# The first query block's first 512 keys under a bound of their own

## The chip, the cores and the metric

One core of one Trainium2 chip. The metric is device microseconds (us) of one execution; a time given here is the median of some executions, and a span is what the profile of one execution covers (about 1.8 us less than its time). Engines: PE multiplies matrices, ACT (ScalarE) does the exponentials, DVE (VectorE) and POOL (GpSimd) do elementwise work, SP issues most transfers. PE leaves its results in banks of PSUM (named PD, PO and PA); ACT and DVE copy them out from there, which the texts call evacuation.

## The reference, cut to what matters

```python
B, S, D, H = 1, 2048, 448, 16          # Dh = 28
qkv = (x @ wqkv).reshape(B, S, 3, H, Dh).transpose(2, 0, 3, 1, 4)
q, k, v = qkv[0], qkv[1], qkv[2]
scores = jnp.einsum("bhqd,bhkd->bhqk", q, k) * (Dh ** -0.5)
p = jax.nn.softmax(scores, axis=-1)
o = jnp.einsum("bhqk,bhkd->bhqd", p, v)
out = o.transpose(0, 2, 1, 3).reshape(B, S, D) @ wo
```

Everything is bfloat16. There are 16 heads x 2048 queries x 2048 keys, so 67 million exponentials.

## The kernel before

Heads are taken in 4 groups of 4, queries in blocks of 512. Scores are computed with keys on the partitions. The kernel does not take the true maximum over keys but an upper bound: for each dimension the largest absolute key value (KMAX) times the absolute query value, summed over the dimensions. The bound rides in the same matmul: each head has 32 spare rows, which hold minus the margin times KMAX on the key side (KB) and |q| on the query side (QB). The exponentials are split: most tiles go to ACT, two at a time (128x1024, named PTA), the others run through a polynomial on DVE and POOL (names DU, DV, DG, PTD).

The consequence for the start: no score can be formed before the maxima of **all** 2048 keys of the group are known, hence not before the whole input has been loaded, transposed and projected to keys.

```python
# setup: four x blocks by SP, weights of K and Q by ACT's queue
for b in range(NQC):
    nc.sync.dma_start(out=XS[b][:], in_=x_perm[:, b * TPC:(b + 1) * TPC, :])
for (W, off) in ((WK, D), (WQ, 0)):
    nc.scalar.dma_start(out=W[:, :, 0:GW], in_=wq3[:, :, off:off + GW])
# ...
nc.vector.memset(maskm[:], -MARG)
nc.vector.tensor_scalar(out=maskm[:], in0=maskm[:], scalar1=maskcol[:, 0:1], ...)
# ... memsets of VA and WO on DVE, then the first transfers of WO

# each x block: PE transposes, DVE copies one half to XT_0, ACT the other to XT_1
# K of group 0, four chunks (sc) of 512 keys: 4 matmuls, maximum on DVE, copy on ACT
red = nc.vector.tensor_reduce(out=KPART[g][:, sc:sc + 1], in_=ap(), op=ALU.max, apply_absolute_value=True)
nc.scalar.activation(out=KB[0][pr][:, cs], in_=ap(), func=ACT.Identity, bias=onescol[:, 0:1], scale=1.0)
# ... after all four chunks
nc.vector.tensor_reduce(out=KMAX[g][:], in_=KPART[g][:], op=ALU.max)
# bound rows of KB (32x512, x4 for the first chunk) and of QB (|q|, x4)
nc.vector.tensor_scalar(out=KB[0][i // 2][...], in0=maskm[...], scalar1=KMAX[g][...], op0=ALU.mult)
nc.vector.tensor_scalar(out=qb[i // 2][...].bitcast(U16), in0=qb[i // 2][...].bitcast(U16), scalar1=0x7FFF, op0=ALU.bitwise_and)
```

The order of instructions on every engine is fixed when the program is built, by a small list scheduler inside the kernel that works with estimated durations (the numbers 0.585, 0.61 and so on in the diff below) and a priority for each operation. A few constants (DI, QEA, PARTU) steer it. A plan is an order and not a clock: if an instruction comes late, all behind it on its engine come late, even if they could have run (in the changed kernel Q's copy on ACT stood behind a K copy that waited 0.82 us for DVE, and started 2.3 us behind the first K copy; with that K copy moved behind it, in run g0, 0.8 us).

## Time and profile before

| | before |
|---|---|
| time, median | 415.06 us; 414.88 beside the changed kernel |
| span of the profiled execution | 413.1 us |
| ACT busy | 400.0 us, 97% |
| first exponential starts | 16.38 us |
| fourth exponential starts | 19.45 us |
| last of 424 exponentials starts / ends | 404.28 / 405.56 us |
| ACT's wait ahead of the last copies | 3.06 us |

The profile's page for the kernel before: span, busy time, ACT and PE clock in 40 slices of the span (9 is 90% or more), and the chain of waits.

```profile
span 413.1 us, 7525 instructions
PE 362.4 (88%) x2605; PEld 121.4 (29%) x2617; DVE 394.0 (95%) x696; ACT 400.0 (97%) x439; POOL 224.1 (54%) x203
...
ACT  4999999999999999999999999999999999999994
...
PEclk9999999999999999999999999999999999999999
...
ACT 86%; issue 8%; PE 2%; DMA 2%; DVE 1%; SPq 0%; DVEq 0%; ACTq 0%
```

ACT is full in every slice but the first and the last, and 86% of the chain that ended last lies on it. So the time is made of three parts: when ACT's stream starts, how much work lies in it, and the tail behind it. DVE at 95% is nearly as full, which is why work cannot simply be handed to it.

ACT's timeline of the kernel before, around the start and at the end. The columns are start and length in us, engine, line, operation, output and input, count, and in brackets how long the engine sat idle before it and what released it.

```profile
14.29 0.69 ACT L474 ACTIVATE QB_0_85<-PD_201,offscol 128x512 bf16<-128x512 f32 x1 [0.24 <-PE PD_201 L466]
...
15.44 0.69 ACT L474 ACTIVATE QB_1_86<-PD_201,offscol 128x512 bf16<-128x512 f32 x1
16.38 1.02 ACT L903 ACTIVATE PTA_131<-PA_198 128x1024 bf16<-128x1024 f32 x1 [0.25 <-PE PA_198 L631]
...
19.45 1.03 ACT L903 ACTIVATE PTA_134<-PA_199 128x1024 bf16<-128x1024 f32 x1
...
404.28 1.28 ACT L903 ACTIVATE PTA_145<-PA_199 128x1024 bf16<-128x1024 f32 x1
408.61 0.53 ACT L1032 CAST OUTF_211<-PD_201 128x448 bf16<-128x448 f32 x1 [3.06 <-PE PD_201 L1027]
```

Exponentials follow each other at 0.917 us (the printed lengths overlap). Before the first ACT makes five K copies and two Q copies (the Q copies at 14.29 and 15.44 are shown, the first held up by PE); behind the last, ACT waits 3.06 us for the last block's normalisation and output matmuls.

DVE's timeline of the same kernel, the setup up to the first transpose copy:

```profile
3.19 0.35 DVE L231 TENSOR_SCALAR maskm<-maskm,maskcol 128x512 bf16<-128x512 bf16 x1
...
4.78 0.81 DVE L234 MEMSET WO<- 128x896 uint32 x1
5.50 0.21 DVE L286 COPY WKP_79<-WK 112x448 bf16<-112x448 bf16 x1
5.66 0.69 DVE L319 COPY XT_0_63<-PD_200 112x1024 bf16<-112x1024 bf16 x1
```

### The profile page before, as it was taken

What the parts mean: (1) busy time and instruction counts of PE and PEld (TensorE: products, weight loads), DVE (VectorE), ACT (ScalarE), POOL (GpSimd) and SP (SyncE); (2) the same over time, 40 slices, a digit from 0 to 9 for tenths busy, and PEclk for the clock granted to TensorE, in tenths of its full rate; (3) what the DMA queues carried; (4) which work ended last, traced back from release to release, by engine and by line L of the source; (5) the groups of instructions that cost most, each with busy time, mean ns of one, the idle gap of its engine ahead of it and who ended that gap; (6) DMA issues with size and microseconds to landing.
All of it is one profiled execution on the core that took longest, in us unless ns stands there. A gap on an engine that the chain in (4) does not pass through costs nothing.

```text
span 413.1 us, 7525 instructions
## 1 busy us (share of the span) xinstructions
PE 362.4 (88%) x2605; PEld 121.4 (29%) x2617; DVE 394.0 (95%) x696; ACT 400.0 (97%) x439; POOL 224.1 (54%) x203
## 2 busy tenths in 40 slices
PE   8988989898898889888898988979898888989995
PEld 4533232223232232322223222222322222222231
DVE  6899999999999999999999999999999999999975
ACT  4999999999999999999999999999999999999994
POOL 2155456464655556475465656547375656556450
PEclk9999999999999999999999999999999999999999
DMA  8410011202201001110400001010310101001012
GB/s 256 77 20 21 3 47 11 53 25 54 72 1 44 2 28 30 20 38 8 111 8 27 21 9 40 2 36 11 77 48 2 47 2 35 12 27 47 4 69 89
DMA packets 33413, 15.83 MB, mean 38 GB/s; under 512 B 26016, under 2 KB 30304, under 8 KB 33376
## 3 DMA queue, kind: packets, MB, share of 16 engines
q1 hardware_dynamic: 32304, 15.05, 14.5%
q8 instruction: 20, 0.33, 0.4%
q10 hardware_dynamic: 1072, 0.32, 0.3%
q14 instruction: 17, 0.14, 0.1%
HBM read 7.37 MB, written 1.96 MB: 23 GB/s over the span
## 4 chain that ended last, share of the span: by engine, by line
ACT 86%; issue 8%; PE 2%; DMA 2%; DVE 1%; SPq 0%; DVEq 0%; ACTq 0%
ACT PTA_131 L903 5%; ACT PTA_132 L903 4%; ACT PTA_133 L903 4%; ACT PTA_136 L903 4%; ACT PTA_135 L903 4%; ACT PTA_134 L903 4%; ACT PTA_145 L903 4%; ACT PTA_140 L903 4%; ACT PTA_139 L903 4%; ACT PTA_138 L903 4%; ACT PTA_137 L903 4%; ACT PTA_144 L903 4%; ACT PTA_142 L903 3%; ACT PTA_143 L903 3%; ACT PTA_141 L903 3%
## 5 line engine op out<-in xcount | busy, mean ns | idle before, releaser
L714 POOL TENSOR_TENSOR DG_181<-DV_175,DU_169 128x512 f16<-128x512 f16 x30 | 34.6, 1155 | 34.8 <-DVE DV_175 L711 34.6
L714 POOL TENSOR_TENSOR DG_182<-DV_176,DU_170 128x512 f16<-128x512 f16 x30 | 34.6, 1155 | 28.8 <-DVE DV_176 L711 28.7
L714 POOL TENSOR_TENSOR DG_184<-DV_178,DU_172 128x512 f16<-128x512 f16 x29 | 33.5, 1155 | 29.5 <-DVE DV_178 L711 28.2
L714 POOL TENSOR_TENSOR DG_186<-DV_180,DU_174 128x512 f16<-128x512 f16 x29 | 33.5, 1155 | 26.9 <-DVE DV_180 L711 26.7
L714 POOL TENSOR_TENSOR DG_185<-DV_179,DU_173 128x512 f16<-128x512 f16 x29 | 33.5, 1155 | 25.7 <-DVE DV_179 L711 25.6
L714 POOL TENSOR_TENSOR DG_183<-DV_177,DU_171 128x512 f16<-128x512 f16 x29 | 33.5, 1156 | 22.9 <-DVE DV_177 L711 22.7
L631 PEld LDWEIGHTS <-KB_1_94 64*128 64x128 bf16 x256 | 20.8, 92 | 48.4 <-issue 47.4
L631 PEld LDWEIGHTS <-KB_0_91 64*128 64x128 bf16 x256 | 20.5, 92 | 45.8 <-issue 42.1
L631 PEld LDWEIGHTS <-KB_1_92 64*128 64x128 bf16 x256 | 20.1, 93 | 45.8 <-issue 44.0
L631 PEld LDWEIGHTS <-KB_0_93 64*128 64x128 bf16 x256 | 20.3, 92 | 43.5 <-issue 42.5
L903 ACT ACTIVATE PTA_140<-PA_199 128x1024 bf16<-128x1024 f32 x18 | 22.4, 1247 | 0.0
L903 ACT ACTIVATE PTA_144<-PA_199 128x1024 bf16<-128x1024 f32 x18 | 22.4, 1245 | 0.0
L903 ACT ACTIVATE PTA_143<-PA_198 128x1024 bf16<-128x1024 f32 x18 | 22.3, 1241 | 0.0
L903 ACT ACTIVATE PTA_142<-PA_199 128x1024 bf16<-128x1024 f32 x18 | 22.3, 1239 | 0.0
L903 ACT ACTIVATE PTA_141<-PA_198 128x1024 bf16<-128x1024 f32 x18 | 22.3, 1236 | 0.0
L903 ACT ACTIVATE PTA_139<-PA_198 128x1024 bf16<-128x1024 f32 x17 | 21.1, 1241 | 0.0
L708 DVE TENSOR_SCALAR DU_171<-PD_202 128x512 f16<-128x512 uint16 x29 | 19.8, 682 | 1.0 <-PE PD_202 L631 0.7
L708 DVE TENSOR_SCALAR DU_172<-PD_200 128x512 f16<-128x512 uint16 x29 | 19.7, 681 | 0.9 <-PE PD_200 L631 0.9
L711 DVE SCALAR_TENSOR_TENSOR DV_178<-PD_200,DU_172 128x512 f16<-128x512 uint16 x29 | 19.8, 684 | 0.3
L711 DVE SCALAR_TENSOR_TENSOR DV_176<-PD_201,DU_170 128x512 f16<-128x512 uint16 x29 | 19.8, 683 | 0.2
L708 DVE TENSOR_SCALAR DU_169<-PD_200 128x512 f16<-128x512 uint16 x29 | 19.8, 682 | 0.2 <-PE PD_200 L631 0.2
L903 ACT ACTIVATE PTA_145<-PA_198 128x1024 bf16<-128x1024 f32 x16 | 20.0, 1247 | 0.0
(596 smaller groups left out, 1511.3 us busy)
## 6 DMA issues: line engine op xcount, KB each, us to landing
RRB_194<-SCR_196 SPq DMA_DIRECT2D x8, 256.0 KB
RRB_195<-SCR_197 SPq DMA_DIRECT2D x7, 256.0 KB
KB_1_94<-KB_0_93 SPq DMA_DIRECT2D x4, 128.0 KB
XS_127<-in_x_dram SPq DMA_DIRECT2D x1, 448.0 KB
XS_128<-in_x_dram SPq DMA_DIRECT2D x1, 448.0 KB
XS_129<-in_x_dram SPq DMA_DIRECT2D x1, 448.0 KB
XS_130<-in_x_dram SPq DMA_DIRECT2D x1, 448.0 KB
out_dram<-XS_127 SPq DMA_DIRECT2D x1, 448.0 KB
```

What stands on the lines that cost most here:

```text
L631: nc.tensor.matmul(out=ap, lhsT=KB[g % 2][i // 2][a:a + 64, j * P:(j + 1) * P], rhs=QB[w % NQB][i // 2][a:a + 64, :], start=True, stop=Tru ...
L708: p1 = add(Op("DVE", P1, lambda: nc.vector.tensor_scalar(out=DU[b][:], in0=lo, scalar1=SIG / 65536, scalar2=SIG * (SS - 0.5), op0=ALU.mult ...
L711: p2 = add(Op("DVE", P1, lambda: nc.vector.scalar_tensor_tensor(out=DV[b][:], in0=lo, scalar=65536 * (SS - 0.5 + CE / C3), in1=DU[b][:], o ...
L714: gq = add(Op("POOL", PTT, lambda: nc.gpsimd.tensor_tensor(out=DG[b][:], in0=DV[b][:], in1=DU[b][:], op=ALU.mult), deps=[p2], prio=n, kind ...
L903: nc.scalar.activation(out=PTA[pslot.idx][:, 0:len(ns) * QW], in_=PA[s.idx][:, 0:len(ns) * QW], func=ACT.Exp, bias=ACT_BIAS, scale=ACT_SCALE)
```

## The change

The intent is to start ACT's stream sooner. For the first query block the first 512 keys run under a bound made of **their own** maxima, so the first exponentials need only one K chunk and Q. The other 1536 keys of the block run under the bound of all maxima, as before. The two parts of the block then have value sums under different bounds; the first part is copied out, multiplied by exp(difference of the bounds), and added to the second.

To make this cheap the factors change sides: KB's bound rows become the constant minus the margin, and the query side holds |q| times the maxima. For group 0 that constant has to be written into four 32x1536 pieces of KB, which is done by POOL. The core of the diff (the cuts are marked; left out are mostly changed priorities and PSUM banks of the plan; Q's weights are now loaded by SP and their copy runs on ACT instead of POOL):

```diff
-    DI = 2
+    DI = 1
...
-    QEA = 30
+    QEA = 20
...
-    PARTU = 40
+    PARTU = 50
...
+    nc.vector.tensor_scalar(out=negm[:], in0=maskm[:, 0:HP], scalar1=-1.0, scalar2=None, op0=ALU.mult)
+    for pr in range(2):
+        for st in range(HG):
+            nc.gpsimd.memset(selcol[pr][HP * st:HP * (st + 1), :], 1.0 if st % 2 == pr else 0.0)
+        nc.vector.tensor_tensor(out=bndcol[pr][:], in0=onescol[:], in1=maskm[:, 0:1], op=ALU.subtract)
+        nc.vector.tensor_tensor(out=bndcol[pr][:], in0=bndcol[pr][:], in1=selcol[pr][:], op=ALU.mult)
+        nc.vector.tensor_tensor(out=bndcol[pr][:], in0=bndcol[pr][:], in1=maskm[:, 0:1], op=ALU.add)
+    for pr in range(2):
+        for st in range(HG):
+            if st % 2 != pr:
+                nc.gpsimd.memset(KB[0][pr][HP * st:HP * (st + 1), QW:S], -MARG)
...
-            evs = [add(Op("ACT", 0.585, lambda pr=pr: nc.scalar.activation(
-                out=KB[0][pr][:, cs], in_=ap(), func=ACT.Identity, bias=onescol[:, 0:1], scale=1.0),
-                deps=[ops[-1], red], ...)) for pr in range(2 if sc == 0 else 1)]
+            if sc == 0:
+                evs = [add(Op("ACT", 0.585, lambda pr=pr: nc.scalar.activation(
+                    out=KB[0][pr][:, cs], in_=ap(), func=ACT.Identity, bias=bndcol[pr][:, 0:1], scale=selcol[pr][:, 0:1]),
+                    deps=[ops[-1]], prio=-4480 if pr == 0 else -4360, lat=0.17)) ... for pr in range(2)]
...
+            else:      # chunks 1 to 3 go through KB[1] and are moved by DMA
+                evs = [add(Op("ACT", 0.585, lambda: nc.scalar.activation(out=KB[1][0][:, cs], ...)))]
...
+            for i in range(HG):    # first 512 keys: |q| times chunk 0's maxima
+                o = bound(qb, i, KPART[0], [ab, kmaxop[0][0], e1], ...)
+            for i in range(HG):    # the rest: |q| times all maxima
+                qev2[i] = bound(q2, i, KMAX[0], [cps[i // 2], ab, kmax_op[0]], ...)
...
+    def task_factor():
...
+        e = add(Op("ACT", 0.49, lambda: nc.scalar.activation(out=DT[:], in_=bank(task)[:], func=ACT.Exp, scale=ACT_SCALE), ...))
...
+    def finish_block():
+        ev = add(Op("DVE", 0.62, lambda: nc.vector.tensor_copy(out=RRB[1][:], in_=PO[:]), ...))
+        first_part.append(add(Op("POOL", 1.22, lambda: nc.gpsimd.tensor_tensor(out=RRB[1][:], in0=RRB[1][:], in1=DT[:], op=ALU.mult), ...)))
...
+            ev = add(Op("DVE", 0.62, lambda: nc.vector.tensor_tensor(out=OSB[b][:], in0=PO[:], in1=RRB[1][:], op=ALU.add), ...))
```

## The prediction

> **What bounds the kernel.** The exponentials on ACT. The page: ACT 97% busy, 86% of the chain that ended last; the stretches of busy time: ACT 100% from 21 to 395 us. In ACT's timeline the first exponential starts at 16.38 us, the 424th at 404.28: 0.917 us each, no gap but 0.33 us after the first. Then 8.8 us of tail. Time = start of the stream + ACT work inside it + tail.
>
> **Removed.** 16.38 us ends a chain: x block 2 lands at 7.94, transposes, all four K chunks (PE done 13.38), the last reduction of maxima (14.19), the overall maximum, two bound writes into KB (0.34 each), two into QB (0.28 each). The first block now needs only K chunk 0 and Q 0. Also gone from ACT before the stream: one transpose copy (0.9), one Q and three K evacuations (0.585 each).
>
> **Added or moved.** By the instruction order: the three K evacuations stand between the first exponentials (3 x 0.6); one exponential of the rescaling factor (about 0.5); 425 exponential pairs, not 424 (0.92), as DVE gets 174 tiles, not 176. Together 3.2 us more ACT work inside the stream. DVE gets seven small setup instructions ahead of the K weight copy (about 1.1 us: dependent DVE instructions follow each other at 0.2 us in the trace), four 32x512 bound multiplies (0.34) twice, copies of Q (0.28), one transpose copy, one copy of the partial sums (0.6), mostly paid for by two tiles fewer (3.6). Tail: same work.
>
> **The new start, by trace durations.** Setup moves XT_0_63 on DVE from 5.66 to about 6.7; K0 is done on PE about 9.1. [...] before's waits agree: ACT waited twice for DVE's maximum of the same bank (0.5 us in all). So evacuation, maximum and second evacuation of that bank alternate, ACT, DVE, ACT: 9.1, 9.8, 10.6. Q's evacuation ends about 11.8; absolute value, copy, a transpose copy and two bounds on DVE end about 13.7; first exponential about 14.1, 2.3 us earlier.
>
> Then the stream is not dense. The second K chunk's maximum stands on DVE behind two more bounds, two transpose copies and a copy, and ACT's next instruction waits for it: a hole of about 1.5 us after exponential 1. The fourth exponential starts about 20.2 (before: 19.45). Moving K chunks by DMA (issue 0.6 each, landing roughly 2 us) should be just in time.
>
> Balance: stream position +0.8, factor +0.5, one more exponential +0.9: +2.2 us by this count. The retuned constants may give some back, and the start is uncertain by 1.5 us, so I lower it to +1.1: 416.2 us, range 412.8 to 418.8. Faster by over 2%: 0.02; within: 0.95; slower: 0.03.
>
> **What would show it.** ACT's timeline: first exponential at 13 to 15 us; ACT idle 1 to 2 us between exponential 1 and the K evacuation, released by DVE's maximum; fourth exponential at 19 to 21; then 0.917 spacing; last exponential starting 8 to 9 us before the end. DVE: XT_0_63 at 6.5 to 7.
>
> **What would make it wrong.** GpSimd's four new memsets (32x1536) holding up DVE's fast copies: start later by 1 us or more. Plan skew: the order was fixed for earlier starts, so PE may hold ACT's scores behind tiles that wait for DVE: holes after 20 us, up to 419. If setup costs DVE less and the hole closes, 413.

The alternation rests on the two waits alone (0.21 and 0.25 us in the trace of the kernel before). The sum: 0.8 + 0.5 + 0.9 = 2.2 us, lowered to 1.1, on 415.06 us. The figures for DMA can be read in the same trace: the first copy of KB, issued at 15.58 us, took 0.63 us to issue, and its packets had landed at 17.46, 1.9 us after the start of the issue.

## More of the kernel before

The granted clock is the share of PE's full speed that the profile records.

The granted clock of PE from 8 to 14 us in the kernel before. The columns are the stretch, its length, busy us of PE, weight loads, DVE, ACT and POOL with counts, the PE clock as a share of full speed, the share of the DMA engines, GB/s.

```profile
8.00:14.00 6.00, 5.84 (x50) 3.66 (x51) 3.87 (x6) 4.91 (x7) 1.33 (x1) 1.00 0.80 155
```

## The result

The changed kernel takes 422.18 us (4 runs, 421.95 to 422.23), the kernel before 414.88 (4 runs, 414.65 to 415.25). The ratio is 1.0176, with a 95% interval of 1.0161 to 1.0190. Ratios here are the mean time of one kernel's runs over that of the other's of the same rounds, so not quite the ratio of the medians. The change made the kernel 1.8% slower; it lies outside the predicted range (412.8 to 418.8).

Its page, the same lines:

```profile
span 420.4 us, 7567 instructions
PE 364.9 (87%) x2617; PEld 122.4 (29%) x2617; DVE 397.3 (94%) x705; ACT 400.5 (95%) x440; POOL 227.7 (54%) x213
...
ACT  2599999999999999999999999999999999999993
...
PEclk8899999999999999999999999999999999999998
...
ACT 74%; PE 12%; DVE 6%; issue 6%; POOL 1%; POOLq 0%; ACTq 0%; DVEq 0%
```

ACT is busy for 400.5 us, only 0.5 more than before: the loss of 7.3 us of span is not work but waiting. It shows in the first slices (2 and 5 where there were 4 and 9), and the PE clock is below full there too. The chain of waits, 86% on ACT before, now runs through PE and DVE for 18%.

ACT's timeline of the changed kernel:

```profile
12.73 0.78 ACT L429 ACTIVATE KB<-PD,bndcol,selcol 128x512 bf16<-128x512 f32 x1 [5.64 <-PE PD L418]
14.33 0.78 ACT L429 ACTIVATE KB<-PD,bndcol,selcol 128x512 bf16<-128x512 f32 x1 [0.82 <-DVE KPART L425]
15.00 0.68 ACT L529 ACTIVATE QB<-PD,offscol 128x512 bf16<-128x512 f32 x1
...
18.03 1.02 ACT L1018 ACTIVATE PTA<-PA 128x1024 bf16<-128x1024 f32 x1 [0.17 <-PE PA L700]
20.60 0.69 ACT L438 ACTIVATE KB<-PD,onescol 128x512 bf16<-128x512 f32 x1 [1.55 <-DVE KPART L425]
...
24.31 1.93 ACT L1018 ACTIVATE PTA<-PA 128x1024 bf16<-128x1024 f32 x2
...
389.49 22.37 ACT L1018 ACTIVATE PTA<-PA 128x1024 bf16<-128x1024 f32 x24
415.75 0.53 ACT L1147 CAST OUTF<-PD 128x448 bf16<-128x448 f32 x1 [3.89 <-PE PD L1142]
```

The first exponential starts at 18.03 us, not 2.3 us earlier than before but 1.65 later. Ahead of it ACT waits 5.64 us for the first K chunk from PE. The 1.55 us hole behind the first exponential was predicted and is there. The last exponential ends at 389.49 + 22.37 = 411.86, and ACT then waits 3.89 us, 0.83 more than before.

The 7.3 us of span divide exactly into three stretches, each read off these timelines:

| stretch | before | after | difference |
|---|---|---|---|
| span's start to the fourth exponential's start | 19.45 | 24.31 | +4.86 |
| from there to the last exponential's end | 386.11 | 387.55 | +1.44 |
| last exponential's end to the span's end | 7.54 | 8.54 | +1.00 |

The middle one is one more exponential (425, 0.92 us) and the exponential of the factor (about 0.5). The three rows are used below as start, work and tail.

Why the first K chunk is so late shows on DVE (the changed kernel's timeline, the instructions shown of before and the new one ahead of them):

```profile
3.20 0.35 DVE L245 TENSOR_SCALAR maskm<-maskm,maskcol 128x512 bf16<-128x512 bf16 x1
3.59 1.31 DVE L246 TENSOR_SCALAR negm<-maskm 128x32 bf16<-128x32 bf16 x1
...
7.13 0.81 DVE L259 MEMSET WO<- 128x896 uint32 x1
7.86 1.42 DVE L311 COPY WKP<-WK 112x448 bf16<-112x448 bf16 x1
9.20 0.67 DVE L350 COPY XT<-PD 112x1024 bf16<-112x1024 bf16 x1
```

and on POOL, in the same stretch:

```profile
3.37 5.77 POOL L256 MEMSET KB<- 32x1536 bf16 x4
```

A multiplication of 128x32 elements took 1.31 us, and the copy of the K weights, 0.21 us before, took 1.42. Both ended just when one of POOL's four memsets of 1.44 us ended: 3.37 + 1.44 = 4.81 against 4.90, and 3.37 + 5.77 = 9.14 against 9.28. The first transpose copy XT_0_63 stands behind them on DVE at 9.20 us instead of 5.66.

And PE, which needs that copy for the first K matmuls, sat idle. The changed kernel's PE timeline and its clock in the stretch shown of before:

```profile
9.92 1.01 PE L418 MATMUL PD<-XT,WKP 112*128 112x512 bf16 x2 [4.34 <-DVE XT L350]
```

```profile
8.00:14.00 6.00, 4.08 (x16) 2.22 (x17) 3.02 (x4) 0.78 (x1) 1.14 (x1) 0.50 0.71 146
```

PE waited 4.34 us, and from 8 to 14 us its granted clock was half of full speed. Two matmuls of the K chunk took 1.01 us where two took 0.60 before.

So there is a chain of three suspects: POOL's memsets hold up DVE's short instructions (0.21 us grew to 1.42); PE idles (4.34 us) and its clock falls (to 0.50); and the plan's order, made for earlier starts, leaves holes. The traces suggest it. The runs below test it.

### The profile page after: what moved, and what is told of

It is laid out like the page before. It is cut to its first block, busy times and chain, and to the rows that moved or that the text cites. A ratio compares the mean times of both kernels' runs of the same rounds, so it can differ in the third digit from the quotient of the medians. Undisturbed runs are those within 1.5% of the kernel's fastest.

```text
span 420.4 us, 7567 instructions
## 1 busy us (share of the span) xinstructions
PE 364.9 (87%) x2617; PEld 122.4 (29%) x2617; DVE 397.3 (94%) x705; ACT 400.5 (95%) x440; POOL 227.7 (54%) x213
## 4 chain that ended last, share of the span: by engine, by line
ACT 74%; PE 12%; DVE 6%; issue 6%; POOL 1%; POOLq 0%; ACTq 0%; DVEq 0%
ACT PTA L1018 73%; PE PA L700 5%; PE PO L871 3%; PE PD L700 1%; DVE DV L816 1%; DVE DU L813 1%; DVE XT L350 1%; PE PO L418 1%; DVE PTD L832 0%; PE PD L418 0%; PE PO L521 0%; PE PO L587 0%; ACT KB L429 0%; DVE QB L541 0%; DVE WKP L311 0%
## 5 line engine op out<-in xcount | busy, mean ns | idle before, releaser
L1018 ACT ACTIVATE PTA<-PA 128x1024 bf16<-128x1024 f32 x425 | 390.5, 1233 | 0.2 <-PE PA L700 0.2
L819 POOL TENSOR_TENSOR DG<-DV,DU 128x512 f16<-128x512 f16 x174 | 200.1, 1154 | 175.3 <-DVE DV L816 151.6
L700 PE MATMUL PA<-QB,KB 64*128 64x512 bf16 x850 | 167.8, 380 | 42.0 <-ACT PTA L1018 39.6
L813 DVE TENSOR_SCALAR DU<-PD 128x512 f16<-128x512 uint16 x174 | 117.9, 681 | 3.5 <-PE PD L700 3.0
L700 PEld LDWEIGHTS <-KB 64*128 64x128 bf16 x1024 | 66.9, 93 | 185.4 <-issue 177.9
L832 DVE SCALAR_TENSOR_TENSOR PTD<-PD,DG 128x512 uint16<-128x512 f32 x174 | 118.0, 680 | 1.3 <-POOL DG L819 0.6
L816 DVE SCALAR_TENSOR_TENSOR DV<-PD,DU 128x512 f16<-128x512 uint16 x174 | 117.7, 682 | 1.1
L871 PE MATMUL PO<-PTA,VA 128*32 128x512 bf16 x850 | 86.3, 386 | 0.3 <-DVE VA L602 0.2
L700 PE MATMUL PD<-QB,KB 64*128 64x512 bf16 x174 | 65.1, 376 | 1.2 <-DVE PTD L832 0.8
L871 PE MATMUL PO<-PTD,VA 128*32 128x512 bf16 x174 | 57.9, 386 | 0.0
```

Source lines behind the costliest of these rows:

```text
L700: nc.tensor.matmul(out=ap, lhsT=KB[g % 2][i // 2][a:a + 64, j * P:(j + 1) * P], rhs=QB[2 if w == 0 and j >= FB else w % NQB][i // 2][a:a + ...
L813: p1 = add(Op("DVE", P1, lambda: nc.vector.tensor_scalar(out=DU[b][:], in0=lo, scalar1=SIG / 65536, scalar2=SIG * (SS - 0.5), op0=ALU.mult ...
L816: p2 = add(Op("DVE", P1, lambda: nc.vector.scalar_tensor_tensor(out=DV[b][:], in0=lo, scalar=65536 * (SS - 0.5 + CE / C3), in1=DU[b][:], o ...
L819: gq = add(Op("POOL", PTT, lambda: nc.gpsimd.tensor_tensor(out=DG[b][:], in0=DV[b][:], in1=DU[b][:], op=ALU.mult), deps=[p2], prio=n, kind ...
L832: f = add(Op("DVE", P1, lambda: nc.vector.scalar_tensor_tensor(out=PTD[st["s"].idx][:].bitcast(U16), in0=PX[slot.idx][:], scalar=EBITS + C ...
L871: nc.tensor.matmul(out=PO[HP * st:HP * (st + 1), :], lhsT=VA[g][:, j, st, :], rhs=r["p"][i][1](), start=first, stop=last, tile_position=(0 ...
```

## The experiments

Fifteen kernels ran, all with right results by the comparison (one of them in spite of a mistake, told below). In the table, the ratio is against the kernel before, run in the same rounds (its medians there lay between 414.63 and 414.92 us). "First" and "fourth" are the starts of these exponentials on ACT, "wait" is ACT's wait ahead of the last copies; all three from the profiled execution.

| run | what differs | time us | ratio | first | fourth | wait |
|---|---|---|---|---|---|---|
| before | | 414.88 | 1 | 16.38 | 19.45 | 3.06 |
| after | | 422.18 | 1.0176 | 18.03 | 24.31 | 3.89 |
| e1_fill_by_dma | after, fills by DMA | 418.46 | 1.0093 | 15.32 | 21.60 | 3.89 |
| e2_dummies | after, 19 dummy matmuls in PE's gap | 421.14 | 1.0161 | 16.95 | 23.24 | 3.89 |
| e3_split_memsets | after, fills in 48 pieces | 419.58 | 1.0117 | 14.56 | 20.84 | 3.89 |
| e4_q_first | after, Q's copy ahead of K's copies | 421.83 | 1.0164 | 18.57 | 24.76 | 3.89 |
| f1_fill_and_dummies | e1, 8 dummies | 418.59 | 1.0106 | 14.48 | 20.77 | 3.89 |
| f2_old_constants | after, the three constants back | 422.30 | 1.0190 | 18.03 | 24.31 | 3.06 |
| f3_short_setup | e1, DVE's setup shortened, 3 dummies | 417.73 | 1.0073 | 14.38 | 20.66 | 3.89 |
| f4_evac_before_max | f1, K copies ahead of K maxima | 419.37 | 1.0109 | 14.98 | 19.42 | 3.89 |
| b1_before_with_fills | before, plus the fills | 414.96 | 1.0001 | 16.51 | 19.60 | 3.06 |
| g0_q_before_second_k | f1, one K copy behind Q's | 417.47 | 1.0064 | 14.17 | 19.97 | 3.89 |
| g1_repaired | all repairs, with a mistake | 417.80 | 1.0076 | 13.87 | 19.88 | 3.89 |
| g2_mended | all repairs, mended | 416.33 | 1.0041 | 13.77 | 18.48 | 3.89 |
| g3_mended_two_old_constants | g2, DI and PARTU back | 416.44 | 1.0046 | 13.92 | 18.63 | 3.91 |
| g4_tail | g2, one late output matmul earlier | 415.81 | 1.0020 | 13.86 | 18.56 | 3.49 |
| g5_tail_and_start | g4, start tightened | 415.08 | 1.0003 | 13.49 | 18.02 | 3.49 |

### Taking the fills off POOL

```diff
-                nc.gpsimd.memset(KB[0][pr][HP * st:HP * (st + 1), QW:S], -MARG)
...
+                nc.sync.dma_start(out=KB[0][pr][HP * st:HP * (st + 1), QW:S].rearrange("p (r q) -> p r q", q=QW),
+                                  in_=maskm[HP * st:HP * (st + 1), None, :].to_broadcast([HP, (S - QW) // QW, QW]))
```

> The four GpSimd fills of KB (5.77 us in the trace of after) are gone; DMA writes the same constants instead. [...] negm falls from 1.31 us to about 0.15 and the K weight copy from 1.42 to 0.22, XT_0_63 on DVE starts at about 6.8 us instead of 9.20, PE waits 1.9 us instead of 4.3 and its clock stays at 1.0 in most of the start; the first exponential comes 2.4 us earlier by the waits alone and about 4.5 us earlier if the clock holds too, near 13.5 to 15.6; time 417.5 to 420. Rival (DVE is simply slow at the start, the fills play no part): the two durations stay, 422.

418.46 us: half of the loss is gone by moving four memsets to DMA. The multiplication that had taken 1.31 us took 0.17, the weight copy 0.21 again, and XT_0_63 started at 6.89 us, close to the predicted 6.7. DVE's timeline of this run:

```profile
3.59 0.17 DVE L246 TENSOR_SCALAR negm<-maskm 128x32 bf16<-128x32 bf16 x1
...
6.77 0.21 DVE L312 COPY WKP<-WK 112x448 bf16<-112x448 bf16 x1
6.89 0.68 DVE L351 COPY XT<-PD 112x1024 bf16<-112x1024 bf16 x1
```

PE still waited 1.91 us for it, and in the profiled execution (419.27 us, span 417.5) the clock was 0.57 of full speed from 8 to 12 us, against the expectation that it would hold; the other three executions had spans of 416.6 and 416.7 and were not traced. So with this wait the clock fell in one execution and, by mean clocks of 0.996 to 0.998 against 0.992, seems to have held in three. In the clock records of the kernel before and of the changed kernel each stretch that ends in a change lasts a whole multiple of 3.41 us (full speed for 406.19 us before; 3.41, 6.83 at half speed and 402.77 in the changed kernel), and they begin with full speed at 5.26 and 4.40 us. What decides whether the clock falls no run tests.

### Keeping PE busy, with the fills left where they were

```diff
+                for n in range(19 if (b, hf) == (0, 1) else 0):
+                    warm(n)          # dummy matmul of zeros, behind the transposes of x block 0
```

> 19 dummy matmuls fill PE's wait between the first transposes and the first K chunk; the GpSimd fills stay. Clock theory: granted clock 1.0 throughout the start instead of 0.50 from 8 to 14 us; K0, transposes and Q0 of 5.0 us (9.92 to 14.34 and on) shrink to about 2.6, first exponential near 16 instead of 18.03, time about 420. XT_0_63 still starts at 9.2 and negm still takes 1.3. Rival (PE's pace at the start is off the chain): first exponential unchanged, 422.

Here DVE's two long instructions are as in the changed kernel (1.31 and 1.42 us; XT_0_63 at 9.19), but PE has no gap. Its clock in the stretch shown twice above:

```profile
8.00:14.00 6.00, 6.00 (x59) 3.93 (x57) 3.25 (x4) 1.52 (x3) 1.14 (x1) 1.00 0.79 152
```

The clock stayed at 1.00, and the first exponential came at 16.95 instead of 18.03: the clock by itself cost 1.08 us, and 1.04 us of time (422.18 to 421.14). The rest of the late start is DVE's, as the run with both repairs shows below.

### The same fill, in small pieces

```diff
-                nc.gpsimd.memset(KB[0][pr][HP * st:HP * (st + 1), QW:S], -MARG)
+                for c0 in range(QW, S, 128):
+                    nc.gpsimd.memset(KB[0][pr][HP * st:HP * (st + 1), c0:c0 + 128], -MARG)
```

> The same GpSimd fills cut into 48 pieces of 32x128. [...] a DVE copy waits for one piece at most, so negm and the K weight copy each wait 0.2 us or less instead of 1.2, although GpSimd is busy as long or longer; start and time like those of the DMA fill (417.5 to 420). Rival (GpSimd work slows DVE in proportion): the waits stay over 1 us, 422.

If POOL merely took bandwidth from DVE, the same bytes in smaller pieces should cost DVE as much. POOL's timeline of this run, then DVE's:

```profile
3.37 7.38 POOL L257 MEMSET KB<- 32x128 bf16 x48
```

```profile
3.59 0.28 DVE L246 TENSOR_SCALAR negm<-maskm 128x32 bf16<-128x32 bf16 x1
...
6.82 0.24 DVE L312 COPY WKP<-WK 112x448 bf16<-112x448 bf16 x1
```

POOL is busy for longer (7.38 instead of 5.77 us, 28% more) and still fills while DVE copies, but DVE's instructions are short: each grew by no more than one piece (0.11 and 0.03 us over e1's, where POOL did not fill). So what DVE sits out here is at most one memset. By what means POOL holds it up is not shown; the lengths are: 1.31 and 1.42 us beside memsets of 1.44 us, 0.28 and 0.24 beside memsets of 0.15 us (7.38 / 48), and DVE's own memset of WO took 0.81 us with the fills (after, e3, b1) and without (before, e1).

The time, 419.58 us, is worse than with DMA. Ahead of the first K copy on ACT the profile shows a wait of 1.20 us and names POOL, but POOL filled on until 10.76 while the copy started at 9.26, and PE's K chunk had ended at 9.17, 0.09 us ahead of the copy just as in f1 below (9.10 and 9.19): the wait was for PE. The first exponential at 14.56 was as early as with the DMA and dummies. In the profiled execution the loss is all behind ACT's last copy (3.7 us to the span's end, 3.0 in f1); what lengthened it there is not shown.

### Q's copy ahead of the K copies

The copies of K chunk 0 (ACT), its maximum (DVE) and the second copy (ACT) read one PSUM bank and ran one after the other: 12.73, 13.54, 14.33. Q's copy stands behind them. Was ACT's order the cost?

```diff
+    for o in (kev[(0, 0, 0)], kev[(0, 0, 2)]):       # both copies of K chunk 0
+        order.remove(o)
+    at0 = order.index(quse[0]) + 1                   # behind Q's copy
+    order[at0:at0] = [kev[(0, 0, 0)], kev[(0, 0, 2)]]
```

> Same plan, but in the emitted order the two evacuations of K chunk 0 on ACT come after the maximum on DVE and after Q's evacuation. Theory that the alternation on one PSUM bank costs: the maximum runs at 12.7 beside no ACT work, Q is evacuated when PE has it (about 14.4 to 15.0 instead of 15.0 to 15.7), then both K evacuations follow without a wait; first exponential 0.5 to 0.8 us earlier, time 421.4 to 421.7. It would gain more (about 1.5) with PE at full clock. Rival (ACT has slack there): no change, 422.2.

My theory fell in this form. The 0.82 us wait was gone, but the first exponential came at 18.57, later than 18.03: Q's copy moved only from 15.00 to 14.38 since PE at half clock delivered Q no earlier, and the two K copies now came after it. 421.83 us against 422.18 is no gain that these rounds can tell from nothing (421.15 to 422.63).

### Fills by DMA and dummies together

```diff
+                for n in range(8 if (b, hf) == (0, 1) else 0):
+                    warm(n)          # on top of the fills by DMA
```

> The DMA fill of e1 plus 8 dummy matmuls in PE's remaining wait of 1.9 us. [...] clock 1.0 throughout (e1 had 0.5 from 8.0 to 11), K chunk 0 done at about 9.1 instead of 9.95, first exponential at about 14.3 instead of 15.32, fourth at about 20.6, time 417.2 to 417.7 against 418.46 of e1. Rival (dummies are worth nothing [...]): 418.5.

A miss in time: 418.59 us, no better than with DMA fills alone (418.46). Three of that run's four executions had already had a nearly full clock (0.996 to 0.998, spans 416.6 to 416.7 as here), so there was little left to win. Nor did the dummies help every time: one of the four executions with them took 420.53 us at a mean clock of 0.990, untraced. But the traced one gives the clean start, with the clock at 1.00 from 8 to 14 us. Its first and fourth exponential on ACT:

```profile
14.48 1.02 ACT L1021 ACTIVATE PTA<-PA 128x1024 bf16<-128x1024 f32 x1 [0.17 <-PE PA L703]
...
20.77 8.34 ACT L1021 ACTIVATE PTA<-PA 128x1024 bf16<-128x1024 f32 x9
```

This splits the late start of the changed kernel: 18.03 - 16.95 = 1.08 us for the clock, 16.95 - 14.48 = 2.47 us for DVE held up by POOL. What remains, 14.48, is the start that the prediction had computed as 14.1.

### The constants

```diff
-    DI = 1
+    DI = 2
...
-    QEA = 20
+    QEA = 30
...
-    PARTU = 50
+    PARTU = 40
```

> The changed kernel with the three retuned constants put back (DI, QEA, PARTU). The plan then gives ACT 426 exponentials instead of 425 and DVE 172 tiles, and ends as in before. Theory: the retuning bought one exponential (0.92 us) with a tail longer by about 0.9, so both cancel: ACT's wait before the last output copies 3.1 us instead of 3.89, time 421.9 to 422.4. Rival (the retuning is what lengthens the end): 421.2 or less.

422.30 us: the same as the changed kernel's 422.18 (against the kernel before, the ratio's interval is 1.0175 to 1.0206, so unclear by the two-per-cent rule). By the order of instructions there are now 426 exponentials instead of 425, and the wait in the tail is 3.06 us instead of 3.89. The retuning had bought one exponential of 0.92 us and paid it back with 0.83 us in the tail. I had counted it as a possible gain.

### A shorter setup on DVE

```diff
-        nc.vector.tensor_tensor(out=bndcol[pr][:], ...)      # six small ones
+        nc.gpsimd.tensor_tensor(out=bndcol[pr][:], ...)
...
+        if o is xt_half[0]:
+            setup_va()       # memsets of VA behind the first transpose copy
+        if o is xt_half[2]:
+            setup_wo()       # memset of WO behind the copy of x block 1
```

> The DMA fill plus a shorter setup on DVE: the six bound-column instructions on GpSimd, the constant fills of VA and WO and negm after the first transpose copies; three dummy matmuls. Theory that DVE's setup is on the chain: XT_0_63 starts at about 5.2 instead of 6.9 (e1), first exponential about 1.2 us earlier than in f1, near 13, fourth near 19.3; time 416.0 to 416.6. If the clock falls all the same, 417. Rival (by then x's second block or WQ is what PE waits for): as f1.

In the trace the rival was mostly right. XT_0_63 started at 5.73 us, 1.2 earlier, and the first exponential at 14.38, 0.1 earlier. The memset of WO had moved in front of the first maximum, so ACT's wait for that maximum grew from 0.82 to 1.07 us, and the transposes of x block 0 took 1.91 us on PE, where the changed kernel's had taken 1.06:

```profile
4.52 1.06 PE L339 MATMUL PD<-ident,XS 128*112 128x128 bf16 x16
```

```profile
4.63 1.91 PE L343 MATMUL PD<-ident,XS 128*112 128x128 bf16 x16
```

The reason is the clock, which the profile's clock column hides: it prints 1.00 for the time ahead of the trace's first clock record. The eight dummies before these transposes start about 427 ns apart (the first two about 380) in the kernel before and in the changed one, against 216 in e2's row of 19 at full speed. The records give full speed from 4.40 us on in the changed kernel and from 6.89 in this run; in the first the transposes start 56 ns apart, in this one 107. In f1, where full speed came at 5.29, the distance changes from 107 to 56 at just that time, and in the kernel before at 5.26. So the traced execution started at half speed; why this one did is not shown. It was also the slowest of this run's four (418.32; the others 417.60 to 417.83, spans 415.8 to 416.0). The median, 417.73 us, is 0.9 better than 418.59, so the shorter setup is worth more than the trace shows.

### The hole after the first exponential

ACT's copy of K chunk 1 waits 1.55 us for DVE's maximum of the same bank. Let ACT copy first and DVE take the maximum afterwards, and let PE compute the chunks earlier:

```diff
+    for sc, n in ((1, 0), (3, 3)):            # matmuls of K chunks 1 and 3 earlier
+        at0 = order.index(acts[n][0])         # ahead of the scores of exponentials 0 and 3
+        order[at0:at0] = k0ops[sc]
+    for sc in range(1, NQC):                  # maximum behind the copy
+        order.insert(order.index(k0ev[sc]) + 1, kmaxop[0][sc])
```

> f1 plus another order around the first exponentials: K chunk 1's matmuls before the first scores, K chunk 3's last before the fourth exponential's scores, and each later chunk evacuated by ACT before DVE takes its maximum. Theory that ACT's hole after exponential 1 (1.54 us in after and in every run so far) comes from DVE's maximum standing behind two copies: hole under 0.3 us, fourth exponential 1.2 to 1.5 us earlier than in f1, time 1.0 to 1.4 us below f1. Rival (PE or the DMA moves of K limit next): the hole moves to exponentials 2 to 6 and the gain is below 0.5.

The hole closed and the time did not follow. ACT's timeline of this run:

```profile
19.42 3.01 ACT L1024 ACTIVATE PTA<-PA 128x1024 bf16<-128x1024 f32 x3
23.27 2.85 ACT L1024 ACTIVATE PTA<-PA 128x1024 bf16<-128x1024 f32 x3 [0.85 <-PE PA L706]
26.71 1.02 ACT L1024 ACTIVATE PTA<-PA 128x1024 bf16<-128x1024 f32 x1 [0.58 <-PE PA L706]
```

The fourth exponential started 1.35 us earlier than in f1 (19.42 against 20.77), and between 23 and 29 us ACT waited 1.8 us for scores. What the next scores hang on had not moved forward with it: all maxima were known on DVE at 20.32 (20.18 in f1), the second bounds were written until 21.95 (21.80), and DVE's first copy of V came behind them; PE stood 0.97 us behind that copy with ACT's scores behind it. The hole had moved. And in this execution the clock fell as well: its records show 0.50 from 25.20 to 28.62 us, so the last two waits, 0.58 and 0.38, lie at half speed. How much of the loss is the order's and how much the clock's is not separated; the untraced execution with the highest mean clock (0.997) had a span of 416.5, level with f1's 416.6. An early fourth exponential is worth nothing if PE's order puts something late ahead of the next scores.

### The disputed cost by itself, in the kernel before

```diff
+    for pr in range(2):
+        for st in range(HG):
+            if st % 2 != pr:
+                nc.gpsimd.memset(KB[0][pr][HP * st:HP * (st + 1), QW:S], -MARG)
```

> The kernel before plus only the four GpSimd memsets of 32x1536 (into a place that is overwritten later, so the result stays right). It measures the disputed cost alone, where the chain has slack. Theory [...]: the K weight copy on DVE, 0.21 us at 5.50 in the kernel before, takes 0.9 us or more or starts 0.7 us or more later; the multiply of the mask at about 3.2 may be held too; XT_0_63 starts up to 1.6 us later than 5.66. But since all K chunks had to wait for x block 2, which landed at 7.94, the first exponential is at most 0.6 us later than 16.38 and the time within 0.6 us of the kernel before. Rival (the memsets cost because of something else in the changed kernel[...]): DVE's instructions keep their lengths and starts within 0.1 us. Should the first exponential move by 1 us or more, the setup was tighter than I read it.

DVE's timeline of this run:

```profile
3.20 0.75 DVE L231 TENSOR_SCALAR maskm<-maskm,maskcol 128x512 bf16<-128x512 bf16 x1
...
5.92 0.91 DVE L290 COPY WKP<-WK 112x448 bf16<-112x448 bf16 x1
```

The same memsets lengthen the same kind of instructions (0.35 to 0.75, 0.21 to 0.91 us), XT_0_63 comes 1.09 us later (6.75), and the time is 414.96: nothing, because there the first exponential has to wait for x block 2 and all K chunks anyhow (16.51 against 16.38). The fills were not dear in themselves. They became dear because the change had put the K weight copy and the first transpose copy on the critical path, and put the fills beside them.

### One copy moved in the clean kernel

```diff
+    order.remove(kev[(0, 0, 2)])                              # second copy of K chunk 0
+    order.insert(order.index(quse[0]) + 1, kev[(0, 0, 2)])    # behind Q's copy
```

> The run with fills by DMA and eight dummies (418.59 us, first exponential 14.48, fourth 20.77), with one move: ACT's second evacuation of the first K chunk (which waits 0.82 us for DVE's maximum in the same PSUM bank) stands after Q's evacuation. Theory (ACT's fixed order puts a wait for DVE in front of Q's evacuation, which the whole chain of bounds hangs on): Q's evacuation starts about 10.0 instead of 11.46, its absolute value on DVE about 10.9, first exponential 0.6 to 1.5 us earlier than 14.48, fourth exponential earlier by as much, time 417.2 to 418.1. Rival (the start is held by PE and by the transposes of x block 2, whose copy is the last thing ahead of the first scores, as the run with Q's evacuation first suggested): first exponential within 0.3 of 14.48 and time 418.4 to 418.8.

417.47 us, 1.1 less than 418.59. Q's copy started 0.8 us behind the first K copy instead of 2.3, so the wait for the maximum of that bank was filled with work. Its start was later than I had expected (10.43, not 10.0): in this execution the transposes of x block 0 took 1.85 us (the records give full speed only from 6.29 us on), and everything started 0.4 us late. The first exponential gained only 0.3 in the trace, the fourth 0.8. What e4, with both K copies moved and at half clock, could not show, shows here.

### All repairs, with a mistake, and mended

```diff
+    move([kev[(0, 0, 2)]], after=quse[0])
+    for sc, n in ((1, 0), (2, 2), (3, 3)):     # matmuls of K chunks 1 to 3 earlier
+        move(k0ops[sc], before=acts[n][0])
+    move([kmaxop[0][1]], before=xt_half[6])    # maximum of chunk 1 ahead of two transpose copies
+    move([kmaxop[0][2]], after=xt_half[7])
...
+            nc.gpsimd.tensor_tensor(...)       # and the shorter setup, WO behind the first maximum
```

> All repairs at once: fills by DMA, seven small setup operations off DVE's way, second evacuation of K chunk 0 after Q's evacuation, matmuls of K chunks 1 to 3 moved ahead of the scores that PE now does before them, and the maximum of chunk 1 ahead of two transpose copies on DVE. Theory (the start and the hole are the whole cost, apart from 1.4 us of added ACT work inside the stream and 1.0 of tail): first exponential 12.6 to 13.5, holes among the first exponentials under 0.7 us together, span 413.6 to 414.5, time 415.3 to 416.3, that is within 0.5 per cent of the kernel before. It should not beat it: with 1.4 + 1.0 us of added work and tail the first exponential plus holes would have to come to under 12.7 us. Rival (moving waits only makes new ones, as in the run with evacuations ahead of the maxima): new waits of ACT on PE's scores of 1 us or more before 30 us, time 417 or more.

417.80 us (416.50 to 419.61) at a span expected at 413.6 to 414.5 and measured at 415.7. ACT still waited 0.89 us for K chunk 2. PE's timeline of this run showed my mistake:

```profile
16.22 1.02 PE L423 MATMUL PD<-XT,WKP 112*128 112x512 bf16 x4 [2.14 <-DVE KPART L432]
```

The matmuls of chunk 2 waited for a *maximum*, which should have waited for them. I had moved the maximum ahead of its matmuls in program order, so it read what chunk 0 had left in that bank. The result still passed the comparison, since the bound need not be exact; the trace told what the comparison could not. The run settles nothing about the theory. Its times spread widely, at mean clocks of 0.988 to 0.999; that this is the start without dummies is likely and not shown, since one execution alone was traced.

Mended, the maximum stands behind the matmuls, and three dummies fill PE's wait for x block 1:

```diff
-    move([kmaxop[0][2]], after=xt_half[7])
+    at0 = max(order.index(k0ops[2][-1]), order.index(xt_half[7]))
+    move([kmaxop[0][2]], after=order[at0])
...
+        if o is k0mm[1]:
+            for n in range(3):
+                warm(n)
```

> The run with all repairs had a mistake of mine: the maximum of K chunk 2 stood ahead of that chunk's matmuls, so it read the old contents of the bank and made the matmuls wait 2.14 us for it. Here it stands behind them, and three dummy matmuls fill PE's wait for x block 1. Theory (start and hole are the whole loss but for 1.4 us of added ACT work in the stream and 1.0 us of tail): first exponential 13.2 to 13.9, no ACT wait above 0.4 us among the first five exponentials, fourth exponential 17.9 to 18.8 (before: 19.45), span 414.2 to 415.1, time 416.0 to 416.9: still 1 to 2 us over the kernel before, because an earlier fourth exponential by about 1.1 us does not pay for 1.4 + 1.0. Rival (the waits only move on, as with the evacuations ahead of the maxima): new ACT waits for PE's scores of 1 us or more between 20 and 35 us, time 417.5 or more.

ACT's timeline of the mended kernel:

```profile
13.77 1.02 ACT L1025 ACTIVATE PTA<-PA 128x1024 bf16<-128x1024 f32 x1 [0.69 <-PE PA L707]
...
18.48 15.69 ACT L1025 ACTIVATE PTA<-PA 128x1024 bf16<-128x1024 f32 x17
...
393.75 12.29 ACT L1025 ACTIVATE PTA<-PA 128x1024 bf16<-128x1024 f32 x13
409.93 1.40 ACT L1175 CAST OUTF<-PD 128x448 bf16<-128x448 f32 x3 [3.89 <-PE PD L1170]
```

416.33 us, span 414.4, as the theory had it. The books close: start 18.48 - 19.45 = -0.97, work (393.75 + 12.29 - 18.48) - 386.11 = +1.45, tail (414.4 - 406.04) - 7.54 = +0.82, sum +1.30, and the span is 1.3 over that of the kernel before. Behind the first exponential the trace names no wait of ACT up to the last one.

### The tail

```diff
-    DI = 1
+    DI = 2
...
-    PARTU = 50
+    PARTU = 40
```

> The mended kernel with DI back at 2 and PARTU back at 40, QEA left at 20 (by the instruction order 425 exponentials, as in the mended kernel). It asks what made the tail 1.0 us longer (ACT's wait ahead of the last copies 3.89 us instead of 3.06 before). With all three constants back the wait was 3.1 but there was one exponential more. Theory (the tail follows the number of exponentials: what ACT no longer does, DVE and PE still have to finish after it): wait 3.9 again, time within 0.4 us of the mended kernel. Rival (the tail follows DI or PARTU): wait about 3.1, time 0.6 to 1.0 us below the mended kernel.

The wait stayed at 3.91 and the time at 416.44. So the longer tail is not DI's or PARTU's doing. That leaves QEA, the third constant that f2 had put back, or the one exponential more that f2 had with it; no run separates these two. The traces of the tail then showed where it came from. Before the change DVE turned to the last block's normalisation (a transpose of 0.72 us) 0.48 us after the last exponential; in the mended kernel 1.33 us after it (407.37 - 406.04), because an addition of the third block's output stood in front, and its PE matmul stood behind the last 14 value matmuls.

```diff
+    last = [o for o in order if o in opmm][-1]                        # that output matmul
+    move([last], before=[o for o in order if o.kind == "V"][-2])      # two rows of value matmuls earlier
```

> The mended kernel (416.33 us, span 414.4) with one PE matmul moved: the last matmul of the third block's output stood behind the last 14 value matmuls, so that DVE's addition of it (0.62 us) came only after the last exponential and stood ahead of the last block's normalisation (in the mended kernel the addition ran at 406.82 and the first transpose of the normalisation at 407.37; before the change that transpose started 0.48 us after the last exponential, after it 1.33). Here that matmul stands two rows of value matmuls earlier. Theory (this placement is the longer tail): the transpose starts 0.5 to 0.8 us after the last exponential, ACT's wait ahead of the last copies about 3.1 to 3.3 us instead of 3.89, span 413.6 to 413.9, time 415.4 to 415.9. Rival (the longer tail comes from the number of exponentials or from the chain of normalisation itself): wait 3.7 or more, time within 0.3 us of 416.3.

415.81 us; the wait fell to 3.49, half of the way to 3.06. The transpose started 0.91 us after the last exponential (407.03 against 406.12) and not 0.5 to 0.8: the addition is earlier but still in front of it. The placement is a part of the cause, shown for 0.40 us of it. That the remaining 0.43 us is the same addition is what the trace suggests, and no run moved it out of the way altogether.

### The start once more

```diff
-        if o is kmaxop[0][0]:
+        if o is qev2[3]:
             setup_wo()                              # memset of WO behind the second bounds
...
+    move(k0ops[1], before=xtr[(3, 1)])              # K chunk 1 ahead of x block 3's last transposes
```

> The former with two more moves at the start: DVE's memset of the output weights (0.81 us, ahead of Q's absolute value at 10.95 us) goes behind the bounds of the whole block's maxima, and the matmuls of K chunk 1 go ahead of the last transposes of x block 3, so that the first scores start earlier. Theory (the first exponential now hangs on DVE's bounds and on PE's order): first exponential 13.2 to 13.5 instead of 13.77, fourth 17.9 to 18.4, time 0.3 to 0.6 us below the former run: 414.9 to 415.6, level with the kernel before (415), not faster by more than 0.5 us. Rival (the earlier first exponential opens a hole after it, because K chunk 1 and its maximum come no earlier): fourth exponential within 0.2 us of 18.48, time within 0.2 us of the former run.

415.08 us against 414.92 for the kernel before in the same rounds: 1.0003, interval 0.9990 to 1.0017, so level with it. The first exponential came at 13.49 and the fourth at 18.02, and no hole opened. This is the best version of the change that I found. By the medians it is 1.7% faster than the changed kernel, and it does not beat the kernel before.

## Why the prediction was wrong

The time was predicted at 416.2 and came out at 422.18, 6.0 us more. The steps, one by one.

1. **"What bounds the kernel" (ACT's exponentials; time = start + work + tail): right.** The three stretches account for the whole difference of the spans, and in every mended version that was booked this way the sum closed.
2. **"The new start, by trace durations": this step failed, by 3.9 us.** "Setup moves XT_0_63 on DVE from 5.66 to about 6.7" was measured at 9.20; "first exponential about 14.1" at 18.03; "the fourth exponential starts about 20.2" at 24.31. The text did name the cause, under what would make it wrong: "GpSimd's four new memsets (32x1536) holding up DVE's fast copies: start later by 1 us or more". But the sum took the small setup instructions and the K weight copy at the 0.2 us of a trace in which no such memset was running beside them; the multiplication took 1.31 us and the copy 1.42. That cost 2.47 us (e2 against f1; seen also in e1, e3 and b1).
3. **PE's clock was not in the prediction at all.** In PE's idle time of 4.34 us the granted clock fell to 0.50, for 6.83 us: 1.08 us more (after against e2, where dummies filled that time and the clock stayed at 1.00 from 8 to 14 us). It fell inside the waits of e4 and f2 too (3.63 and 3.58 us). The records of the changed kernel put the fall at 7.81 us, 2.2 us after the last transpose, and its end at 14.64. PE had not been idle for all of the time: in the 3.41 us before the fall it was busy for 1.18 us in the changed kernel, for 1.50 in e1 (longest wait 1.91 us) and for 1.84 in f4 (longest wait 0.97 us). A prediction that moves PE's first real work later than its warm-up matmuls has to ask this.
4. **The rest of the start was right.** With both costs out of the way (f1), XT_0_63 came at 6.89 (predicted 6.7), the three accesses to the bank of K chunk 0 at 9.19, 10.00 and 10.79 (predicted 9.1, 9.8, 10.6), the first exponential at 14.48 (14.1), the hole was 1.55 us (1.5), the fourth exponential at 20.77 (20.2). The alternation ACT, DVE, ACT was drawn from two waits of 0.5 us in all before the change; the traces agree as far as they can, with waits of 0.82 us for the maximum of the same bank in every run that kept this order (1.07 in f3, where a memset stood ahead of the maximum). What would happen if both engines read the bank at once no run shows.
5. **"Together 3.2 us more ACT work inside the stream": right in what was added.** The factor and the one exponential measured +1.44 from the fourth exponential on (0.5 + 0.92 predicted); the three K copies lie ahead of it.
6. **"Tail: same work" and "the retuned constants may give some back ... I lower it to +1.1": wrong.** The tail got 1.0 us longer. The constants gave back one exponential, already counted in the 425, and took as much in the tail (f2). The unshaved count of +2.2, plus the tail of 0.8 to 1.0, comes to 3.0 to 3.2; the clean run f1 measured +3.5 in span (416.6 - 413.1).
7. **"Plan skew ... holes after 20 us": did not happen in the changed kernel.** It did happen when I closed the hole by force (f4), with the clock's fall added.

The sum: 4.1 us of start (24.31 - 20.2), 1.0 of tail and 1.1 of shaving make 6.2, against 6.0 missed; the kernel before was 0.2 us faster in these rounds.

Where the expected gain went: the change gains about 1.0 us of start if all its waits are cleared (g2; 1.4 in g5), and costs 1.4 us of ACT work and 0.4 to 0.8 us of tail. Even in g2 the first exponential is only 2.6 us earlier than before (13.77 against 16.38), and by the fourth 1.0 us of that is left, because three K copies of 0.6 us now stand between the first exponentials instead of ahead of them. So the idea worked as intended, and what it gained was about what it cost.

What stays open: what decides whether the clock falls at a short wait; whether it fell in the slower untraced executions of f1 and g1, as their times suggest; and the second half of the tail.

## What to carry to other kernels

When a change puts an instruction on the critical path, cost it in its new surroundings: an "idle" engine filling memory in 1.44 us pieces made 0.2 us copies of DVE take 1.4 us, and the same fill was free where there was slack. Ask also whether the change leaves PE idle in the start, where its clock may fall (to 0.50 here, in a wait of 4.34 us). And before you credit an earlier start, count what the trick adds to the stream and follow the plan to its end: a hole closed in one place opened in another until every engine's order was redone, and the tail moved too.
